# Window attention issued by pairs of steps, and later weight pieces, in an attention-and-router kernel

## The chip, the cores and the metric

One core of a Trainium2 chip runs the whole program. The metric is the device time of one execution in microseconds (us), and of several executions the median. Engines are named as in the profile: PE (TensorE matmul), DVE (VectorE), ACT (ScalarE), POOL (GpSimd), SP (SyncE, which here only issues DMAs).

## What is computed

The reference is an attention with a local window of 96 positions and 8 global keys, followed by a mixture of experts in which every token goes to one of 8 experts.

```
scores = q @ k.T / sqrt(D) - slopes * dist        # keep: key < 8, or 0 <= query - key < 96
a      = softmax(scores);  x = (a @ v) as (B*S, H*D)    # 4 batches, 8 heads, 768 positions, D 64
logits = (x / |x|) @ (emb / |emb|).T / tau        # 3072 tokens, 8 experts
e      = argmax(logits);  out = max(prob) * relu(x @ w1[e]) @ w2[e]     # 512 -> 1024 -> 512
```

All of it is float32.

## The kernel before

The program has two stages. In the first, `window_attention`, the 32 (batch, head) pairs are worked through in eight groups of four heads; two groups make a batch. Keys are cut in eight blocks of 96 rows, each with 30 rows of global keys under it (126 rows in all); a block with its queries is a unit, two units are a step, and four steps are a group, so there are 32 steps, numbered 0 to 31. In the last batch (steps 24 to 31) the steps of the two groups alternate. The order of PE, ACT, DVE and SP is the order in which the code is written; POOL's is left to a scheduler.

A step does the following on PE. `score` multiplies the keys and queries of its two units (32 small matmuls, L485) into two PSUM tiles a unit. `turn` transposes q and k of a coming group (three transposes a piece, L460), up to eight pieces a group. Then come the pieces of a half batch that is finished (`half_turns`): `turn_x` transposes a tile of 128 tokens (L587), `turn_sums` the row sums (L555), `turn_products` the experts' scores (L573), and `choose` counts the tokens of an expert (L219, L222). Last comes `attend` for the step before: exponentials times v (L514), and on every second step the row sums (L524), and, where a half batch is done, `score_experts` (L564).

Every PSUM tile for scores and transposes comes from `bank()`, which hands out five banks in turn, pa_121 to pa_125: whoever takes a bank waits until the engine that reads its former content is done. For scores that is ACT, which takes the exponential (`grow`, L491; DVE then multiplies by the window table, `weigh`, L498); for pieces of q and k it is ACT too (L462, L465, and the spread of the global keys, L467); for a token tile it is DVE (`store_x`, L596, which multiplies by the reciprocal row sums of L558 and so can't run before them); for the row sums DVE (L558), for the experts' scores DVE (L577, L579). `store_x` writes into one of three tiles xs, has SP store it to x_dram, and has ACT square it (L601). The squares go to POOL for a square root (`choose`, L226), from there to DVE (L236 to L238) and to ACT (L241).

SP issues, in program order, the loads of q, k and v of the group after the next (a quarter a step), the stores of xs, and the expert weights in pieces of 128 KB: from step 11 one in the middle and one at the end of each step. Expert 0 has 32 pieces (16 of w1, 16 of w2); the weights of expert 1 follow from step 27 on, when the tiles of q and k are given up.

The end of `window_attention` finishes the last half batch, issues what is left of expert 1's w1 with one call, `weights_part(count)`, and gives the rest to the second stage, which issues it behind the gathers of expert 0's tokens. The second stage runs the experts one after the other (gathers on POOL, products on PE).

Of the kernel before, what the change touches and what calls it, by code (L numbers as in the profile page):

```python
# [20 lines left out]
P = 128  # L21
# [11 lines left out]
BLK = 96  # L33
# [348 lines left out]
def window_attention(k, ctx):  # L382
# [5 lines left out]
    def pool(name, bufs, **kw):  # L388
# [5 lines left out]
    qk_p, tmp = (early.enter_context(tc.tile_pool(name=name, bufs=n, side="right"))  # L394
                 for name, n in (("wa_qk", 4), ("wa_tmp", 1)))
# [6 lines left out]
    k.junk, lS = (h[:, 0:2, :].rearrange("p f n -> p (f n)") for h in k.first.hT)  # L402
# [66 lines left out]
    def score(u):  # L469
# [5 lines left out]
        u.ex = (late_p if u.late else ex_p).tile([P, 2, 2, 2 * BLK], F32, name="ex", tag="ex")  # L475
# [24 lines left out]
    def attend(g, p, split=True):  # L500


        if p % 2 == 0:
            g.od = [po_p.tile([P, 512], F32, name="od%d" % i, tag="od%d" % i) for i in range(3)]
            k.free = g.od[2][:, QB * BLK :]
# [13 lines left out]
        g.parts = parts = (g.parts if p % 2 else []) + parts  # L519
        for u, at, c0, c1, first in parts if p % 2 else []:  # L520
            for a in range(2):
                for e in range(2):
# [3 lines left out]
                                     skip_group_check=True)  # L526
        if p % 2:
            xd = xd_p.tile([P, 2, QB * BLK], F32, name="xd", tag="xd")
            nc.scalar.copy(out=xd[:, 1, :], in_=g.od[1][:, 0 : QB * BLK])
            (nc.vector.tensor_copy if split else nc.scalar.copy)(out=xd[:, 0, :], in_=g.od[0][:, 0 : QB * BLK])  # L530
            g.xd.append(xd)
            h, den = p // 2, g.batch.den
            if g.m == 0:
                den[h] = den_p.tile([P, QB * BLK], F32, name="den", tag="den")
                nc.vector.tensor_copy(out=den[h][:], in_=g.od[2][:, 0 : QB * BLK])
            else:
                nc.vector.tensor_tensor(out=den[h][:], in0=g.od[2][:, 0 : QB * BLK], in1=den[h][:], op=ALU.add)
# [22 lines left out]
    def score_experts(hf, ps):  # L560
# [5 lines left out]
        nc.scalar.copy(out=lS[:, 0 : 3 * P], in_=ps[:, 0 : 3 * P])  # L566

    def turn_products(hf):
# [3 lines left out]
        for c in range(3):  # L572
            nc.tensor.transpose(ps[:, c * P : (c + 1) * P], lS[:, c * P : (c + 1) * P], k.ident[:])  # L573
# [47 lines left out]
    def half_turns(hf):  # L621
# [5 lines left out]
        elif hf.phase == 1:  # L627
# [4 lines left out]
        if hf.router and hf.phase == 1:  # L632
# [58 lines left out]
    for g in groups:  # L691
        g.units = []
        for j in range(NB):
            u = Net()
            u.g, u.j, u.n = g, j, (2 * BLK if j < NB - 1 else BLK)
            u.late = g.b == B - 1 and j == QB - 1
# [68 lines left out]
    waiting, active, k.root = [], [], []  # L765
    weights = [(0, i) for i in range(PIECES)]
    for s, (g, p) in enumerate(steps):
        if s % 8 == 0:
            before = t if s else None
            pair = groups[s // 4 : s // 4 + 2]  # L770
            t = new_batch(g.b)
            t.groups = pair
            for x in pair:
                x.batch = t
        ahead = s // 4 + 2
        if ahead < len(groups):
            if s % 4 == 0:
                open_group(groups[ahead])
            load_part(groups[ahead], s % 4)
        if s == len(steps) - 5:  # L780
            early.close()
            k.w.append(new_weights(k, k.second_weights()))
            weights.extend((1, i) for i in range(PIECES))

        def weights_part(n=1):
            for _ in range(n):
                if s >= 11 and weights:
                    e, i = weights.pop(0)
                    load_weights_part(k, e, k.w[e], i)

# [3 lines left out]

        us = g.units[2 * p : 2 * p + 2]
# [1045 lines left out]
```

## Time and profile before

| what | us |
|---|---|
| median of three runs | 512.15 |
| the three runs | 513.62, 508.52, 512.15 |
| the profiled execution, its own time | 511.49 |
| its span, first to last instruction | 509.8 |
| steps 4 to 23, scoring of step 4 to scoring of step 24 | 29.04 to 123.24 |
| steps 24 to 31, to the end of the last row sums on PE | 123.24 to 168.49 |

The span is the time between the first and the last instruction in the trace; 1.7 us of the execution's own time lie around it. Times in the rows below are microseconds from the start of the span. Matmuls overlap at their ends, so what a piece costs on PE is read from its start to the start of the next piece, not from its own length.

### The profile page before, as it was taken

How to read it: one execution, taken by the hardware profiler on the slowest of the kernel's cores; microseconds unless marked ns; L12 is line 12 of the kernel's file. 1: busy time of each engine (PE TensorE's matmuls, PEld its weight loads, DVE VectorE, ACT ScalarE, POOL GpSimd, SP SyncE). 2: the span in 40 equal slices, each digit the busy share in tenths (PEclk: the TensorE clock that was granted, in tenths of full speed). 3: DMA queues.
4: the chain of work that ended last, by engine and by line, in shares of the span. 5: the costliest groups of instructions: out<-in, count | busy, mean ns of one | idle time of the engine just before them, and what ended most of it. 6: DMA issues, size and time to landing. Idle time of an engine off the chain costs nothing.

```text
span 509.8 us, 13673 instructions
## 1 busy us (share of the span) xinstructions
PE 487.8 (96%) x5510; PEld 402.1 (79%) x5510; DVE 325.8 (64%) x642; ACT 183.2 (36%) x445; POOL 239.3 (47%) x265
## 2 busy tenths in 40 slices
PE   8999999999989898999999999999989989999995
PEld 7777887887867687969788579899779679859964
DVE  5646777766778565858569636777756664727531
ACT  4967867867654321402112111222212211312220
POOL 4211131333362526376736743865865764843022
PEclk9999999999999999999999999999998999999998
DMA  8999999799743636729561255284382274111001
GB/s 163 204 199 171 212 229 217 185 225 204 193 84 62 199 57 148 205 62 348 195 223 32 69 195 196 67 275 153 119 294 66 50 268 152 50 67 59 0 23 68
DMA packets 112863, 76.34 MB, mean 150 GB/s; under 512 B 88517, under 2 KB 96709, under 8 KB 112721
## 3 DMA queue, kind: packets, MB, share of 16 engines
q1 hardware_dynamic: 103057, 59.00, 44.1%
q0 software_dynamic: 8064, 15.27, 9.7%
q8 instruction: 63, 1.03, 0.9%
q14 instruction: 79, 0.65, 0.4%
q10 hardware_dynamic: 1600, 0.39, 0.4%
HBM read 61.66 MB, written 17.16 MB: 155 GB/s over the span
## 4 chain that ended last, share of the span: by engine, by line
PE 23%; issue 17%; POOL 13%; DMA 6%; POOLq 2%; DVE 1%; ACT 0%
PE big L1347 10%; POOL out_dram L1300 7%; DMA xg<-x_dram,squares 5%; POOL xg L1030 5%; PE big L1153 4%; PE work L1281 3%; PE big L1324 2%; PE work L1072 1%; PE work L1153 1%; POOLq L1806 1%; DMA xg<-x_dram,idss 1%; PE work L1062 0%; POOL landed L1029 0%; PE work L1294 0%; POOL xg L1003 0%
## 5 line engine op out<-in xcount | busy, mean ns | idle before, releaser
L1030 POOL DMA_INDIRECT xg<-x_dram,squares x96 | 107.1, 1116 | 62.5 <-issue 44.4
L498 DVE TENSOR_TENSOR ex<-ex,table 126x768 f32<-126x768 f32 x64 | 60.4, 950 | 36.7 <-ACT ex L491 36.5
L1347 PE MATMUL big<-xT,w1t 128*128 128x160 f32 (+4 forms) x336 | 61.2, 337 | 4.3 <-ACT hT L1371 2.3
L1347 PEld LDWEIGHTS big<-xT,w1t 128*128 128x128 f32 x336 | 56.4, 195 | 7.5 <-issue 2.8
L1357 DVE TENSOR_TENSOR hT<-big,hT 128x320 f32<-128x320 f32 (+4 forms) x70 | 38.4, 562 | 35.8 <-PE big L1347 26.7
L491 ACT ACTIVATE ex<-pa 126x384 f32<-126x384 f32 (+1 forms) x128 | 53.3, 477 | 16.4 <-PE pa L485 15.6
L261 POOL DMA_INDIRECT meta<-mt,slot x24 | 27.3, 1139 | 41.3 <-DVE rd L558 15.8
L514 PE MATMUL od<-ex,v 126*64 126x192 f32 (+1 forms) x576 | 46.0, 305 | 0.0
L1359 ACT ACTIVATE hT<-hT 128x320 f32<-128x320 f32 (+4 forms) x42 | 22.1, 531 | 57.1 <-DVE hT L1357 57.1
L514 PEld LDWEIGHTS od<-ex,v 126*64 126x64 f32 x576 | 34.7, 136 | 7.5 <-issue 3.5
L435 POOL COPY v<-v 30x896 f32<-30x896 f32 (+1 forms) x15 | 17.2, 1158 | 48.0 <-DMA v<-in_v_dram 28.5
L1347 PE MATMUL big<-xsum,fsum 128*128 128x160 f32 (+4 forms) x224 | 39.6, 330 | 0.0
L485 PE MATMUL pa<-qT,kT 64*32 64x128 f32 (+3 forms) x2048 | 38.2, 268 | 0.3 <-DVE xs L596 0.2
L485 PEld LDWEIGHTS pa<-qT,kT 64*32 64x32 f32 (+1 forms) x2048 | 29.7, 107 | 10.9 <-issue 7.2
L1347 PEld LDWEIGHTS big<-xsum,fsum 128*128 128x128 f32 x224 | 36.3, 190 | 1.7 <-DVE fsum L1117 0.4
L1300 POOL DMA_INDIRECT out_dram<-y_arm,tids x17 | 19.6, 1153 | 36.4 <-ACT y_arm L1283 31.8
L1281 PE MATMUL work<-w2t,hT 128*128 128x512 f32 x80 | 35.1, 593 | 0.0
L1153 PE MATMUL big<-wsum,hsum 128*128 128x256 f32 x136 | 31.2, 380 | 0.7 <-DVE hsum L1117 0.4
L1039 DVE STREAM_TRANSPOSE xT<-xg 128x512 f32<-128x512 f32 x24 | 25.3, 1082 | 7.6 <-DMA xg<-x_dram,squares 7.6
L1153 PEld LDWEIGHTS big<-wsum,hsum 128*128 128x128 f32 x136 | 25.7, 190 | 5.3 <-issue 1.1
L1153 PE MATMUL big<-w2t,hT 128*128 128x256 f32 x112 | 27.8, 386 | 1.3 <-DVE hsum L1118 1.0
L1281 PEld LDWEIGHTS work<-w2t,hT 128*128 128x128 f32 x80 | 15.1, 190 | 17.7 <-issue 17.6
(250 smaller groups left out, 871.1 us busy)
## 6 DMA issues: line engine op xcount, KB each, us to landing
w1t<-in_moe_w_dram SPq DMA_DIRECT2D x24, 512.0 KB, 7.4
w2t<-in_moe_w_dram SPq DMA_DIRECT2D x6, 2048.0 KB, 9.6
v<-in_v_dram SPq DMA_DIRECT2D x32, 192.0 KB, 4.4
x_dram<-xs SPq DMA_DIRECT2D x23, 256.0 KB, 4.7
k<-in_k_dram SPq DMA_DIRECT2D x28, 192.0 KB, 5.1
q<-in_q_dram SPq DMA_DIRECT2D x28, 192.0 KB, 5.5
w1t<-in_moe_w_dram SPq DMA_DIRECT2D x32, 128.0 KB, 5.8
w2t<-in_moe_w_dram SPq DMA_DIRECT2D x32, 128.0 KB, 3.4
```

What stands on the lines that cost most here:

```text
L261: i = nc.gpsimd.indirect_dma_start(out=k.meta[:], out_offset=bass.IndirectOffsetOnAxis(ap=slot[:, t : t + 1], axis=0), in_=mt[:, t, :], in ...
L485: i = nc.tensor.matmul(u.sp[e][k0:k1, a * n + c0 : a * n + c1], lhsT=t.kT[rows, j, k0:k1], rhs=t.qT[rows, j * BLK + c0 : j * BLK + c1], st ...
L491: nc.scalar.activation(u.ex[:, e], u.sp[e][0:ROWS, 0 : 2 * u.n].rearrange("p (a c) -> p a c", a=2), AF.Exp, scale=k.scale)
L498: nc.vector.tensor_tensor(out=exv, in0=exv, in1=tab[:, :, 0 : u.n // BLK, :], op=ALU.mult)
L514: nc.tensor.matmul(g.od[a][e * D : (e + 1) * D, at : at + c1 - c0], lhsT=g.v[0:ROWS, 2 * a + e, u.j, :], rhs=u.ex[:, e, a, c0:c1], start=f ...
L1030: k.nc.gpsimd.indirect_dma_start(out=xgs[j][:, g * P : (g + 1) * P], out_offset=None, in_=src, in_offset=bass.IndirectOffsetOnAxis(ap=ids[ ...
L1039: k.nc.vector.transpose(out=xT[:, :, :, j * half : (j + 1) * half].rearrange("p c a (g i) -> p g c a i", i=LACE), in_=xgs[j][:].rearrange( ...
L1153: i = self.k.nc.tensor.matmul(ps, lhsT=x[:, f, :], rhs=w[:, f, :], start=f == 0 and not add, stop=True, skip_group_check=True)
L1281: nc.tensor.matmul(ps[:], lhsT=hT[:, f, j * P : (j + 1) * P], rhs=w2[:, f, :], start=i == 0, stop=i == k.NF - 1)
L1300: i = k.nc.gpsimd.indirect_dma_start(out=k.out.rearrange("t (i m) -> (t i) m", i=n), out_offset=bass.IndirectOffsetOnAxis(ap=ids, axis=0), ...
L1347: nc.tensor.matmul(to[f // 2][:, f % 2 * 256 : f % 2 * 256 + h], lhsT=x[:, l, f * P : (f + 1) * P], rhs=y[:, l, 0:h], start=not (add or f ...
L1357: nc.vector.tensor_tensor(out=to, in0=x, in1=z, op=ALU.add)
```

## The change

Steps 4 to 23 are issued two at a time by a new function, `double`; steps 0 to 3 and 24 to 31 keep the old form, `single`. A double scores its first two units, does the values of the two steps of the double before, scores the other two, does the row sums, then the experts' scores if a half batch is done, then all pieces of q and k of both steps, then the pieces of finished halves. Where a step has its own pieces in the old form, a double does two token tiles in a row.

```
+    def double(s):
+        ...
+        score(us[0])
+        score(us[1])
+        exps(us[0])
+        exps(us[1])
+        done = [steps[i] for i in undone]
+        for q, qp in done:
+            values(q, qp)
+        copy_values(q, s < len(steps) - 10)
+        weights_part(s)
+        score(us[2])
+        scored = score(us[3])
+        scatter_later(k, 2, [scored] + k.root)
+        exps(us[2])
+        sums(q)
+        exps(us[3])
+        copy_sums(q, qp // 2)
+        undone[:] = [s, s + 1]
+        fresh = halves_done(done)
+        for x, a, i in turns[s] + turns[s + 1]:
+            turn(x.pairs[a], i)
+        for hf in active:
+            if hf.phase > hf.count:
+                half_router(hf)
+                hf.phase += 1
+                continue
+            for _ in range(2 if hf.h == 0 else 1 if hf.phase == 0 else 3):
+                half_turns(hf)
+                hf.phase += 1
+            if hf.router and hf.phase > hf.count:
+                next(hf.router)
+        active[:] = still(active) + fresh
+        weights_part(s)
+
+    for s in range(4):
+        single(s)
+    for s in range(4, 8 * (B - 1), 2):
+        double(s)
+    for s in range(8 * (B - 1), len(steps)):
+        single(s)
```

`attend` is cut into `values`, `sums`, `copy_values` and `copy_sums`, with the same instructions. The experts' scores have a buffer for each half, so that both can wait at once, and the products are turned right behind the row sums. Four units of a double and those of the double before need nine tiles ex in place of seven; two more come from the memory of the first tables.

```
-    k.junk, lS = (h[:, 0:2, :].rearrange("p f n -> p (f n)") for h in k.first.hT)
+    k.junk, *scored = (k.first.hT[i][:, j : j + 2, :].rearrange("p f n -> p (f n)") for i, j in ((0, 0), (1, 0), (1, 2)))
...
-        u.ex = (late_p if u.late else ex_p).tile([P, 2, 2, 2 * BLK], F32, name="ex", tag="ex")
+        more = k.spare is not None and u.n_th % 9 >= 7
+        u.ex = (late_p if u.late else k.spare if more else ex_p).tile([P, 2, 2, 2 * BLK], F32, name="ex", tag="ex")
...
         if hf.phase == 0:
             turn_sums(hf)
-        elif hf.phase == 1:
             turn_products(hf)
...
-            hf.router.send(bank() if hf.t.b >= B - 2 else k.free)
+            hf.router.send(bank())
```

The weights: a double issues two pieces (one a step), a single four. So 12 pieces go out in steps 12 to 23, 20 in steps 24 to 28, and 12 of expert 1 in steps 29 to 31. The call at the end of `window_attention` is not changed, but the function now takes the step first, and it issues nothing for steps under 11; the four pieces of expert 1's w1 that are left then fall to the second stage.

```
-        def weights_part(n=1):
+    def weights_part(s, n=1):
...
-        weights_part()
+        weights_part(s, 2)
...
     weights_part(sum(i < PIECES // 2 for e, i in weights))
```

What moves is seen first on PE. Before, this is step 16 behind its scoring: L460 are pieces of q and k, L587 a token tile, L573 the experts' scores, L514 and L524 the values and sums of step 15, and L485 the scoring of step 17.

```order
L460 MATMUL pa_122<-ident,k 128x128 x3
L460 MATMUL pa_123<-ident,q 128x128 x3
L587 MATMUL pa_124<-ident,xd 128x128 x4
L573 MATMUL pa_125<-ident,fhT_119 128x128 x3
L514 MATMUL od_1666<-ex,v 64x192 x2
L514 MATMUL od_1667<-ex,v 64x192 x2
L514 MATMUL od_1666<-ex,v 64x96 x2
L514 MATMUL od_1667<-ex,v 64x96 x2
L524 MATMUL od_1668<-ex,halves 32x96 x4
L524 MATMUL od_1668<-ex,halves 32x192 x12
L524 MATMUL od_1668<-ex,halves 32x96 x4
L485 MATMUL pa_121<-qT,kT 32x128
```

Now, on the same engine, this is the end of the double of steps 16 and 17: L581 are the experts' scores, L461 the four pieces, L604 the token tiles, L572 the row sums, L590 the turned scores, and L487 the first two matmuls of the next double's scoring.

```order
L581 MATMUL pa_125<-xd,enb 32x384 x4
L461 MATMUL pa_121<-ident,k 128x128 x3
L461 MATMUL pa_122<-ident,q 128x128 x3
L461 MATMUL pa_123<-ident,q 128x128 x3
L461 MATMUL pa_124<-ident,k 128x128 x3
L604 MATMUL pa_125<-ident,xd 128x128 x4
L572 MATMUL pa_121<-ident,den 128x128 x3
L590 MATMUL pa_122<-ident,fhT_119 128x128 x3
L604 MATMUL pa_123<-ident,xd 128x128 x4
L487 MATMUL pa_124<-qT,kT 32x128
L487 MATMUL pa_125<-qT,kT 32x128
```

Values and sums no longer stand between the transposes and the next scoring, and the second matmul of that scoring takes bank pa_125, the one of the first token tile. On DVE the same place reads, from the last two multiplications by the window table (L500) on: the copy of the sums (L547), reciprocals (L575), experts' scores (L594, L596), the two token tiles (L613), and the first units of the next double.

```order
L500 TENSOR_TENSOR ex<-ex,table 126x768 x2
L547 TENSOR_TENSOR den<-od_1717,den 128x384
L575 RECIPROCAL rd<-pa_121 128x3x4 x2
L594 TENSOR_TENSOR lh<-pa_122,rd 128x192
L596 TENSOR_REDUCE lg<-lh 128x24
L613 TENSOR_TENSOR xs<-pa_125,rd 128x512
L613 TENSOR_TENSOR xs<-pa_123,rd 128x512
L500 TENSOR_TENSOR ex<-ex,table 126x768 x2
```

The token tile in pa_125 is read behind the reciprocals and the experts' scores. On POOL, the place in the last batch where the square roots of batch 2's halves (L226, three columns) stand was this: copies of the global rows of v (L435) and stores of slots (L261) around them.

```order
L261 DMA meta<-mt_2352,slot_2347 28672x3 x3
L435 COPY v<-v 30x2x448
L261 DMA meta<-mt_2352,slot_2347 28672x3 x2
L435 COPY v<-v 30x2x448
L226 TENSOR_TENSOR ss<-ss,half 128x3
L261 DMA meta<-mt_2352,slot_2347 28672x3
L261 DMA meta<-mt_2786,slot_2781 28672x3 x2
L226 TENSOR_TENSOR ss<-ss,half 128x3
```

and is now this, with the copies of v ahead of the slots:

```order
L436 COPY v<-v 30x2x448 x2
L261 DMA meta<-mt_2401,slot_2396 28672x3 x6
L226 TENSOR_TENSOR ss<-ss,half 128x3 x2
L261 DMA meta<-mt_2859,slot_2854 28672x3 x3
L261 DMA meta<-mt_2954,slot_2949 28672x3 x3
```

No copy of v stands before the first square root any more, except those ahead of six stores of slots.

## Rows read from the trace of the kernel before

**Rows 1.** Busy time by stretch: start and end, its length, busy us (and count) of PE, PEld (weight loads), DVE, ACT, POOL, the granted PE clock, the DMA engines' busy share and GB/s.

```profile
29.04:123.24 94.20, 94.05 (x2270) 75.58 (x2268) 65.79 (x135) 65.90 (x173) 23.76 (x21) 1.00 0.94 208
123.24:164.28 41.04, 37.38 (x891) 29.34 (x887) 29.25 (x85) 25.67 (x69) 17.66 (x16) 1.00 0.53 120
...
383.50:386.90 3.40, 3.40 (x13) 3.40 (x12) 1.36 (x2) 0.49 (x1) 1.98 (x3) 0.50 0.20 58
```

**Rows 2.** Waits of PE between 29.04 and 164.28, the two longest: who waited for whom, us in all, times, the longest.

```profile
PE pa L219 <- ACT ex L491: 2.1, 1, 2.1
PE pa L587 <- ACT ex L491: 0.6, 1, 0.6
```

**Rows 3.** Timeline of PE: start, us, engine, line, operation, output<-inputs, shapes, count of records (two to a matmul), and the idle time before it with what ended it. Steps 8 and 9, the end of step 15, one row of step 30, and two of an expert.

```profile
46.60 1.13 PE L485 MATMUL pa<-qT,kT 64*32 64x128 f32 x64
47.66 0.55 PE L460 MATMUL pa<-ident,k 128*128 128x128 f32 x3
48.04 0.49 PE L460 MATMUL pa<-ident,q 128*128 128x128 f32 x3
48.37 0.60 PE L587 MATMUL pa<-ident,xd 128*128 128x128 f32 x4
48.81 0.49 PE L573 MATMUL pa<-ident,fhT 128*128 128x128 f32 x3
49.23 1.20 PE L514 MATMUL od<-ex,v 126*64 126x192 f32 x16
50.36 1.51 PE L524 MATMUL od<-ex,halves 126*32 126x96 f32 x40
51.80 1.13 PE L485 MATMUL pa<-qT,kT 64*32 64x128 f32 x64
...
54.10 1.52 PE L514 MATMUL od<-ex,v 126*64 126x192 f32 x16
55.55 1.13 PE L485 MATMUL pa<-qT,kT 64*32 64x128 f32 x64
...
83.97 0.85 PE L564 MATMUL pa<-xd,enb 128*32 128x384 f32 x8
84.75 1.19 PE L485 MATMUL pa<-qT,kT 64*32 64x128 f32 x64
...
156.97 0.66 PE L485 MATMUL pa<-qT,kT 64*32 64x128 f32 x32 [0.19 <-DVE xs L596]
...
382.77 4.55 PE L1347 MATMUL big<-xT,w1t 128*128 128x192 f32 x16 [2.29 <-ACT hT L1371]
387.15 2.76 PE L1347 MATMUL big<-xsum,fsum 128*128 128x192 f32 x16
```

**Rows 4.** Timeline of DVE, the same columns: a token tile of step 7, the experts' scores and a token tile of step 11, reciprocals and a token tile of step 29, and the sums of expert 1's w1.

```profile
44.74 0.69 DVE L596 TENSOR_TENSOR xs<-pa,rd 128x512 f32<-128x512 f32 x1 [0.20 <-DVE rd L558]
...
64.04 0.36 DVE L577 TENSOR_TENSOR lh<-pa,rd 128x192 f32<-128x192 f32 x1 [0.18 <-PE pa L573]
64.43 0.51 DVE L579 TENSOR_REDUCE lg<-lh 128x24 f32<-128x192 f32 x1
64.84 0.69 DVE L596 TENSOR_TENSOR xs<-pa,rd 128x512 f32<-128x512 f32 x1
...
155.89 0.30 DVE L558 RECIPROCAL rd<-pa 128x12 f32<-128x12 f32 x2
156.23 0.69 DVE L596 TENSOR_TENSOR xs<-pa,rd 128x512 f32<-128x512 f32 x1
...
214.31 1.16 DVE L1115 TENSOR_TENSOR fsum<-w1t 128x1024 f32<-128x1024 f32 x1
```

**Rows 5.** ACT by line and shape between 37 and 124: count, busy us, mean ns of one, idle time before.

```profile
L462 ACT COPY kT<-pa 128x384 f32<-128x384 f32 x19 | 9.7, 510 | 0.0
...
L467 ACT COPY kT<-kT 128x240 f32<-128x240 f32 x9 | 3.5, 393 | 0.3
```

**Rows 6.** Timeline of SP, whose rows are issues of DMAs: first load of step 4, what follows the loads of steps 4 and 5, the first store of a token tile, and the weights of expert 1 behind the gathers.

```profile
38.38 0.97 SPq L425 DMA_DIRECT2D k<-in_k_dram  x2
...
45.39 0.83 SPq L792 DMA_DIRECT2D x_dram<-zrow  x1
...
53.81 0.38 SPq L600 DMA_DIRECT2D x_dram<-xs  x1
...
201.59 9.97 SPq L182 DMA_DIRECT2D w2t<-in_moe_w_dram  x16
```

**Rows 7.** DMA issues by line: engine, count, KB each, median us from issue to landing.

```profile
x_dram<-xs SPq DMA_DIRECT2D x23, 256.0 KB, 4.7
...
w1t<-in_moe_w_dram SPq DMA_DIRECT2D x32, 128.0 KB, 5.8
```

**Rows 8.** Timeline of four engines in step 27, where PE waits longest.

```profile
141.07 0.93 POOL L435 COPY v<-v 30x896 f32<-30x896 f32 x1 [2.92 <-issue]
...
142.08 1.57 POOL L226 TENSOR_TENSOR ss<-ss,half 128x3 f32<-128x3 f32 x1
...
143.68 0.17 DVE L236 TENSOR_SCALAR ss<-ss 128x3 f32<-128x3 f32 x1 [0.78 <-POOL ss L226]
...
144.31 0.22 ACT L241 ACTIVATE lg<-lg 128x24 f32<-128x24 f32 x1 [2.28 <-DVE lg L238]
...
144.97 0.40 PE L219 MATMUL pa<-oh,prefix 128*128 128x24 f32 x2 [2.06 <-ACT ex L491]
```

More of the change, by code (lines that the diff above doesn't have):

```diff
@@ L498, in weigh, with open_sums, values @@
         nc.vector.tensor_tensor(out=exv, in0=exv, in1=tab[:, :, 0 : u.n // BLK, :], op=ALU.mult)
-    def attend(g, p, split=True):
+    def open_sums(g):
+        g.od = [po_p.tile([P, 512], F32, name="od%d" % i, tag="od%d" % i) for i in range(3)]
+        k.free = g.od[2][:, QB * BLK :]
+        g.parts = []
+    def values(g, p):
         if p % 2 == 0:
-            g.od = [po_p.tile([P, 512], F32, name="od%d" % i, tag="od%d" % i) for i in range(3)]
-            k.free = g.od[2][:, QB * BLK :]
+            open_sums(g)
         parts = []
@@ L526, in attend, with copy_values, copy_sums @@
                                      skip_group_check=True)
-        if p % 2:
[L528 to L537, printed above, removed]
+    def copy_values(g, split=True):
+        xd = xd_p.tile([P, 2, QB * BLK], F32, name="xd", tag="xd")
+        nc.scalar.copy(out=xd[:, 1, :], in_=g.od[1][:, 0 : QB * BLK])
+        (nc.vector.tensor_copy if split else nc.scalar.copy)(out=xd[:, 0, :], in_=g.od[0][:, 0 : QB * BLK])
+        g.xd.append(xd)
+    def copy_sums(g, h):
+        den = g.batch.den
+        if g.m == 0:
+            den[h] = den_p.tile([P, QB * BLK], F32, name="den", tag="den")
+            nc.vector.tensor_copy(out=den[h][:], in_=g.od[2][:, 0 : QB * BLK])
+        else:
+            nc.vector.tensor_tensor(out=den[h][:], in0=g.od[2][:, 0 : QB * BLK], in1=den[h][:], op=ALU.add)
+    def attend(g, p, split=True):
+        values(g, p)
+        if p % 2:
+            sums(g)
+            copy_values(g, split)
+            copy_sums(g, p // 2)
     def new_batch(b):
@@ L763, in window_attention, with begin_step @@
             turns[s].append(x)
-    waiting, active, k.root = [], [], []
+    active, undone = [], []
+    k.root, k.spare, k.batch = [], None, None
     weights = [(0, i) for i in range(PIECES)]
-    for s, (g, p) in enumerate(steps):
-        if s % 8 == 0:
[L769 to L774, printed above, removed]
+    def weights_part(s, n=1):
+        for _ in range(n):
+            if s >= 11 and weights:
+                e, i = weights.pop(0)
+                load_weights_part(k, e, k.w[e], i)
+    def begin_step(s, g):
+        if s % 8 == 0:
+            k.before, k.batch = k.batch, new_batch(g.b)
+            k.batch.groups = groups[s // 4 : s // 4 + 2]
+            for x in k.batch.groups:
+                x.batch = k.batch
         ahead = s // 4 + 2
@@ L779, in window_attention @@
             load_part(groups[ahead], s % 4)
+        if s == 4:
+            opening.close()
+            k.spare = early.enter_context(tc.tile_pool(name="wa_ex2", bufs=2, side="right"))
         if s == len(steps) - 5:
+            k.spare = None
             early.close()
@@ L793, in window_attention, with halves_done, still, single @@
             empty_slots(k)
+    def halves_done(done):
+        fresh = []
+        for q, qp in done:
+            if q.m == 1 and qp % 2:
+                fresh.append(start_half(q.batch, qp // 2))
+                score_experts(fresh[-1], bank())
+        return fresh
+    def still(hfs):
+        return [hf for hf in hfs if hf.phase < (hf.count + 2 if hf.router else 3)]
+    def single(s):
+        g, p = steps[s]
+        begin_step(s, g)
         us = g.units[2 * p : 2 * p + 2]
@@ L855, in window_attention @@
     scatter_later(k, len(k.later))
+    t, before = k.batch, k.before
     hf = start_half(t, 1)
```

47 lines of the change are left out of this document (25 added, 22 removed).

## The prediction

> **What bounds the kernel now.** I read the windows by stretch first. In steps 4 to 23, the part that the change rewrites, PE is busy 94.05 of 94.20 us at the full granted clock; DVE and ACT are busy some 66 us each, so each has 28 us to spare, but not always at the right moment [rows 1]. In the last batch PE is busy 37.38 of 41.04 us. The list of PE's waits says where: one wait of 2.1 us, one of 0.6, and smaller ones of about a microsecond together [rows 2]. So the first 20 steps are PE's own work in a row, and a change can win there only by making that work shorter, and lose by making PE wait where it never waited. The DMA engines are 94% busy in that stretch at 208 GB/s [rows 1], yet no wait of PE names a load.
>
> The timeline of PE gives the price of each piece, from its start to the next start [rows 3]: scoring 1.06 us (46.60 to 47.66), a piece of q or k 0.33, a token tile 0.44, row sums or turned scores 0.33, values of a second or fourth step 1.13 (49.23 to 50.36), of a first step 1.45 (54.10 to 55.55), row sums 1.44 (50.36 to 51.80), experts' scores 0.78.
>
> **What the change takes from PE.** It removes no instruction; it puts equal ones beside each other. From rows 3, what a border costs: the values of a first step have 8 matmuls of 192 columns and take 1.45; those of a second or fourth step have 4 of 192 and 4 of 96 and take 1.13. Two run at a time, so 2 x 96 columns cost 0.32, the shorter block's 6 x 96 cost 0.96, and 0.17 are paid once per block. The change joins ten pairs of such blocks (nine doubles, and step 24, which does two steps' values); the first double has one step's values to do. That is 10 x 0.17 = 1.7 us. For the transposes: the first in a group takes 0.38 and the last before values 0.42, where a middle one takes 0.33, so a group costs 0.14 more than its pieces. Steps 5 to 24 had 20 groups, the change leaves 11: 9 x 0.14 = 1.3 us. How transposes are followed by scoring directly is shown by no row; if that border costs the 0.17 of a values block and not 0.09, 11 x 0.08 = 0.9 us come back, and if nothing, another microsecond goes. Together -3.0 us, between -2.1 and -4.0.
>
> **Where PE will wait.** Now the cover that is gone. Before, values and sums (1.13 + 1.44 us) lay between the transposes and the next scoring, and in that time DVE read the token tiles out of their banks; PE never waited for it in steps 4 to 23. In a double, scoring comes directly behind, and it needs four of the five banks. Take the double of steps 16 and 17, times from the start of its transposes: four pieces to 1.37, first token tile 1.37 to 1.81 (bank pa_125), row sums to 2.14, turned scores to 2.47, second token tile to 2.91, and with 0.09 for the border scoring could begin at 3.00. DVE is free, but its chain starts with the row sums: three transposes end 0.49 after their start [rows 3], here at 2.30, and I allow 0.1 until DVE begins. Reciprocals 0.34, scores 0.39 and 0.41, tile 0.69 [rows 4]: 2.40, 2.74, 3.13, 3.54, 4.23. PE goes on 0.05 after a tile's end (156.23 + 0.69 against 156.97) [rows 3, 4], at 4.28, so it waits 1.28. The same double in batch 0 is that of steps 8 and 9.
>
> In the doubles of steps 10 and 18 the first token tile is that of the older half, whose reciprocals are known; the second comes behind the row sums. Counted as above from the start of the transposes: tiles at 1.37 and 1.81, row sums 2.25, scores 2.58, ready at 3.00; one unit scores (0.53), and the second unit wants the second tile's bank at 3.53. DVE: row sums end 2.74, reciprocals 2.84, scores 3.18 and 3.57, tile 3.98 to 4.67, PE at 4.72: a wait of 1.19. In steps 12 and 20 both tiles come early and the counting of tokens behind them covers DVE, so nothing. In 14 and 22 only pieces come: ACT copies them in 0.51 each and needs 0.39 for the spread [rows 5], each start a tenth or so ahead of the last one's end; the third is out at about 2.2, PE asks at 1.46 + 0.53 = 1.99: 0.2 to 0.3. Sum: 2 x 1.28 + 2 x 1.19 + 2 x 0.25 = +5.4 us. The lower bound is 0, as in the stretch now; the upper is 12.8, ten doubles at the longest wait. I take 5.4, since every part of it is a row and the order of the banks is written down.
>
> **Stores of token tiles.** They have three buffers. The tile of 44.74 was written by 45.43 and its store issued at 53.81 [rows 4, 6], since SP was still putting out loads: 8.4 us late. Landing takes 4.7 [rows 7], so a buffer may be held for 13.1 us. A double writes two tiles, so a buffer comes up again after 9.9 us in steps 8 to 10. There SP must put out the eight loads of steps 8 and 9 first, 6.9 us by those of steps 4 and 5 (38.38 to 45.3) [rows 6], behind the 53.8 at which it is done with the older ones: store at 60.7, landed at 65.4. With the doubles of steps 4 and 6 some 14.2 us long, the next user of the buffer comes at about 64.3. That is +0.9 on DVE and so on PE, between 0 and 3.3. Later SP has less to do, since the doubles carry 12 pieces of weights instead of 26: 14 x 128 KB is 1.8 MB or 9 us at 208 GB/s.
>
> **The last batch.** The wait of 2.06 in step 27 is read backwards [rows 8]: counting waits for a bank, that for an exponential on ACT, ACT stands behind L241 until 144.31, that waits for DVE, DVE at 143.68 for the square root on POOL, and POOL began it at 142.08 because a copy of v stood before it in its order and ended at 142.00. The change has no copy of v there, and takes this half one step later, so the square root has a step's time. I count the wait as gone: -2.06, bounds 0 and -2.06. Of the smaller waits of steps 28 to 31, which hang on the same late square roots, half: -0.5, bounds 0 and -1.0. The 0.6 in step 24 stays: four pieces and a token tile follow its scoring as before.
>
> **The weights** I cost at nothing. Expert 0's last piece goes out in step 28, 30 us before its sums; expert 1's last four pieces of w1 go out behind the gathers, from 201.59 on, 0.62 each (9.97 / 16), and land 5.8 later [rows 6, 7], at about 210; DVE wants them at 214.31 [rows 4]. If that cover is gone, every microsecond beyond some 216 is one on the end. The second stage is otherwise untouched and moves as a whole.
>
> **Sum.** -3.0 + 5.4 + 0.9 - 2.06 - 0.5 = +0.7 us. On the profiled execution's 511.49 that is 512.2; its time is 0.66 under the median of the three runs, which themselves lie 5 us apart, so this is a forecast of no change. About 1%, 5.1 us, is what a measurement of this kernel can tell.
>
> **Rivals.** First, faster: the bank waits don't come, since DVE gets to the tiles sooner than my chain, and all small waits of the last batch go: -3.0 - 2.06 - 1.0, which gives 505.4. For it speaks that DVE and ACT are idle for 30% of that stretch; against it the order, in which the tile stands behind four operations that cannot begin before the row sums. Second, slower, by the stores: if SP stays as late as at 53.81, a buffer is held 13.1 us and wanted after 9.8, so DVE stands still for 3.3 us and PE behind it. At steps 10 and 18 that makes 6.6 in place of 0.9: 517.9; also at 12 and 20 it would be 525. It decides from the point where SP is over 5 us behind when the tiles are written. For it speaks the DMA share of 94%; against it the lighter weights.
>
> Third, the clock. The granted clock was 0.50 between 383.50 and 386.90 [rows 1], after PE had been idle for 2.29 us up to 382.77; the block that followed took 4.38 us where the next has 2.76 [rows 3], some 1.7 lost. The idle time of 2.06 in step 27 stood in a stretch granted 1.00, so a wait of 1.3 alone should not do it. But such a wait would now follow 3 us of transposes. Four such drops cost 4 x 1.7 = 6.8: 519.0. The Trainium skill (TensorE: Matmul & The Clock Gate, Part 4: PE-mode transpose) says that transposes don't count as busy for the clock in the same way; by that rule the doubles of steps 8, 10, 16 and 18 would lower it. The wait of 0.6 behind the transposes of step 24 [rows 2] fell in a stretch granted 1.00 [rows 1], so the trace bears the rule out little so far. Fourth, the late pieces of w1 land after 216 and hold up expert 1: up to some 5 us, 517.
>
> **How the numbers follow.** Forecast 0.60, faster rival 0.20, stores 0.13, clock 0.04, weights 0.03. Two thirds of the faster rival lie beyond 1%, and a twentieth of the forecast on each side: faster 0.17. Slower: most of the stores, the clock, half of the weights and that twentieth: 0.18. The rest, 0.65, is within 1%. The range reaches to the faster rival and just over the cheaper form of the second and the clock: 505 to 520; the forecast's own range is 508 to 516.
>
> **What would show it.** In the trace after: no wait of PE for a load; waits of scoring for DVE's token tile, about 1.2 to 1.3 us, in the doubles of steps 8, 10, 16 and 18 and none in 12 and 20; DVE never idle for a buffer but once near 64; the step-27 wait gone; the granted clock 1.00 up to the second stage; steps 4 to 24 some 3 us longer and the rest of the batch some 2.5 shorter. The forecast is wrong if the doubles run without waits, if DVE waits for stores, or if the second stage changes its length by over 2 us.

## The result, and the profile after

The changed kernel takes 515.11 us (median of 20 runs, 511.43 to 518.72), the kernel before, beside it, 512.22 (20 runs, 508.52 to 517.51): a ratio of 1.0063, 95% interval 1.0038 to 1.0088, so some 3 us more. The forecast was 512.2, between 505 and 520, with no change beyond 1% as the likeliest case. The time lies there, but 2.9 us over the forecast, and in the two profiles the excess comes mainly from one place that the forecast's sum doesn't hold.

First the two windows that answer to [rows 1]: steps 4 to 23, and from there to the last values; then the stretch on PE behind its longest wait.

```profile
28.72:124.77 96.05, 90.34 (x2239) 74.67 (x2237) 64.52 (x124) 65.16 (x169) 21.68 (x20) 1.00 0.93 197
124.77:165.06 40.29, 39.57 (x920) 31.44 (x919) 31.60 (x97) 27.27 (x75) 15.56 (x16) 1.00 0.60 133
175.09:181.06 5.97, 5.93 (x19) 4.92 (x20) 2.81 (x9) 3.24 (x8) 3.06 (x4) 0.52 0.74 265
```

Steps 4 to 23 went from 94.20 to 96.05 us, with PE idle for 5.7 of them where it was idle for 0.15; the next stretch from 41.04 to 40.29. The waits of PE, as in [rows 2], name the places:

```profile
PE pa L487 <- DVE xs L613: 4.4, 4, 1.2
PE pa L691 <- DVE xs L613: 3.0, 1, 3.0
...
PE od L531 <- issue: 1.2, 1, 1.2
```

The first row is the four waits that were forecast. This is PE's timeline at the ends of the doubles of steps 8 and 10 (compare the steps of [rows 3]):

```profile
53.40 0.60 PE L604 MATMUL pa<-ident,xd 128*128 128x128 f32 x4
53.84 0.49 PE L572 MATMUL pa<-ident,den 128*128 128x128 f32 x3
54.17 0.49 PE L590 MATMUL pa<-ident,fhT 128*128 128x128 f32 x3
54.50 0.60 PE L604 MATMUL pa<-ident,xd 128*128 128x128 f32 x4
55.03 0.40 PE L487 MATMUL pa<-qT,kT 64*32 64x128 f32 x2
56.43 1.11 PE L487 MATMUL pa<-qT,kT 64*32 64x128 f32 x62 [1.00 <-DVE xs L613]
...
65.23 0.65 PE L487 MATMUL pa<-qT,kT 64*32 64x128 f32 x32
67.06 0.66 PE L487 MATMUL pa<-qT,kT 64*32 64x128 f32 x32 [1.19 <-DVE xs L613]
```

In the first double one matmul of the next scoring gets through and the second stands; in the other a whole unit gets through. Both are as the order of the banks said, and steps 16 and 18 repeat them (1.00 and 1.19). DVE's side of the first wait, in the order of [rows 4]:

```profile
54.44 0.32 DVE L575 RECIPROCAL rd<-pa 128x12 f32<-128x12 f32 x2 [1.59 <-PE pa L572]
54.89 0.36 DVE L594 TENSOR_TENSOR lh<-pa,rd 128x192 f32<-128x192 f32 x1
55.28 0.50 DVE L596 TENSOR_REDUCE lg<-lh 128x24 f32<-128x192 f32 x1
55.70 1.28 DVE L613 TENSOR_TENSOR xs<-pa,rd 128x512 f32<-128x512 f32 x2
```

DVE stands idle for 1.59 us for the row sums, then runs the chain, tile last.

The wait of 2.06 in step 27 [rows 8] is gone: both counts of tokens stand behind a tile without a gap.

```profile
142.07 0.30 PE L219 MATMUL pa<-oh,prefix 128*128 128x24 f32 x2
...
147.41 0.30 PE L219 MATMUL pa<-oh,prefix 128*128 128x24 f32 x2
```

What no part of the forecast has is the tail, behind the last values. PE there, before:

```profile
170.24 1.04 PE L587 MATMUL pa<-ident,xd 128*128 128x128 f32 x8
172.52 1.09 PE L675 MATMUL pa<-ident,xg 128*128 128x128 f32 x8 [1.24 <-DVE xs L596]
173.44 0.49 PE L573 MATMUL pa<-ident,fhT 128*128 128x128 f32 x3
174.33 1.99 PE L683 MATMUL pa<-fxT,w1t 128*128 128x256 f32 x8 [0.40 <-ACT fxT L676]
```

and after:

```profile
171.02 1.04 PE L604 MATMUL pa<-ident,xd 128*128 128x128 f32 x8
175.09 1.97 PE L691 MATMUL pa<-ident,xg 128*128 128x128 f32 x8 [3.04 <-DVE xs L613]
176.86 0.84 PE L590 MATMUL pa<-ident,fhT 128*128 128x128 f32 x3
177.74 3.49 PE L699 MATMUL pa<-fxT,w1t 128*128 128x256 f32 x8
```

PE comes 0.77 us later and waits 3.04 in place of 1.24; then its clock is granted at half (0.52 in the third window above), and the same rows, up to the rest of the first products, take 6.78 us (175.09 to 181.87) in place of 4.86 (172.52 to 177.38). That is 1.80 + 1.92 = 3.7 us. What DVE waits for there is a square root on POOL; POOL's timeline, before:

```profile
156.64 0.96 POOL L261 DMA_INDIRECT meta<-mt,slot  x1 [3.54 <-PE pa L564]
157.90 0.96 POOL L261 DMA_INDIRECT meta<-mt,slot  x1 [0.30 <-issue]
159.17 1.53 POOL L261 DMA_INDIRECT meta<-mt,slot  x1 [0.30 <-issue]
165.58 0.19 POOL L668 CAST ids<-emt 128x4 int32<-128x4 f32 x1 [4.88 <-DMA emt<-meta]
166.57 1.02 POOL L1003 DMA_INDIRECT xg<-x_dram,ids  x1 [0.80 <-POOL ids L668]
167.89 0.97 POOL L1003 DMA_INDIRECT xg<-x_dram,ids  x1 [0.30 <-issue]
168.88 0.90 POOL L226 TENSOR_TENSOR ss<-ss,half 128x3 f32<-128x3 f32 x1
```

and after:

```profile
157.66 0.96 POOL L261 DMA_INDIRECT meta<-mt,slot  x1 [1.70 <-issue]
158.92 0.96 POOL L261 DMA_INDIRECT meta<-mt,slot  x1 [0.30 <-DVE m L205]
160.18 0.96 POOL L261 DMA_INDIRECT meta<-mt,slot  x1 [0.31 <-issue]
161.45 0.96 POOL L261 DMA_INDIRECT meta<-mt,slot  x1 [0.30 <-DVE ex L500]
168.15 0.19 POOL L684 CAST ids<-emt 128x4 int32<-128x4 f32 x1 [5.74 <-DMA emt<-meta]
169.14 1.02 POOL L1088 DMA_INDIRECT xg<-x_dram,ids  x1 [0.81 <-DMA w1t<-in_moe_w_dram]
170.46 0.97 POOL L1088 DMA_INDIRECT xg<-x_dram,ids  x1 [0.30 <-issue]
171.45 0.90 POOL L226 TENSOR_TENSOR ss<-ss,half 128x3 f32<-128x3 f32 x1
```

The slots (L261) of batch 2's second half must be stored, loaded again (emt) and cast before the first gathers (L1088) can go, and the square root stands behind those. All of it is 2.57 us later: four slots stand in the last row in place of three, since the older half of that batch is now taken a step later. The load of the slots on SP, before and after:

```profile
163.69 0.38 SPq L993 DMA_DIRECT2D emt<-meta  x1
...
166.04 0.38 SPq L1078 DMA_DIRECT2D emt<-meta  x1
```

From the start of step 29's scoring PE reaches the wait 20.18 us later before (151.10 to 171.28) and 17.95 after (154.10 to 172.05); the first gather starts 15.47 and 15.04 behind it. PE got 2.2 us shorter there, the chain 0.4.

### The profile page after: what moved, and what is told of

It reads as the page before. It is cut to its first block, busy times and chain, and to the rows that moved or that the text cites. A ratio compares the mean times of both kernels' runs of the same rounds, so it can differ in the third digit from the quotient of the medians.

```text
span 513.1 us, 13684 instructions
## 1 busy us (share of the span) xinstructions
PE 486.7 (95%) x5510; PEld 404.2 (79%) x5510; DVE 326.8 (64%) x642; ACT 184.4 (36%) x445; POOL 239.0 (47%) x265
## 3 DMA queue, kind: packets, MB, share of 16 engines
q8 instruction: 63, 1.03, 0.9%
## 4 chain that ended last, share of the span: by engine, by line
PE 44%; issue 6%; POOL 5%; DMA 4%; DVE 1%; POOLq 1%; ACT 0%; ACTq 0%
PE big L1432 21%; PE big L1238 9%; PE work L1366 7%; POOL out_dram L1385 3%; PE work L1238 3%; POOL xg L1115 2%; DMA xg<-x_dram,squares 2%; PE big L1409 2%; PE work L1379 1%; PE work L1157 1%; DMA out_dram<-y,idss 1%; DMA xg<-x_dram,idss 1%; PE work L1147 0%; POOLq L1891 0%; POOL landed L1114 0%
## 5 line engine op out<-in xcount | busy, mean ns | idle before, releaser
L1115 POOL DMA_INDIRECT xg<-x_dram,squares x96 | 105.9, 1104 | 60.9 <-issue 42.2
L500 DVE TENSOR_TENSOR ex<-ex,table 126x768 f32<-126x768 f32 x64 | 58.9, 951 | 30.2 <-ACT ex L493 30.0
L493 ACT ACTIVATE ex<-pa 126x384 f32<-126x384 f32 (+1 forms) x128 | 50.8, 479 | 5.9 <-PE pa L487 3.7
L261 POOL DMA_INDIRECT meta<-mt,slot x24 | 26.1, 1089 | 40.6 <-DVE mt L260 12.9
L520 PE MATMUL od<-ex,v 126*64 126x192 f32 (+1 forms) x576 | 43.8, 303 | 0.0
L487 PE MATMUL pa<-qT,kT 64*32 64x128 f32 (+3 forms) x2048 | 39.3, 264 | 4.6 <-DVE xs L613 4.4
L487 PEld LDWEIGHTS pa<-qT,kT 64*32 64x32 f32 (+1 forms) x2048 | 29.0, 105 | 13.5 <-DVE xs L613 5.7
```

Source lines behind the costliest of these rows:

```text
L261: i = nc.gpsimd.indirect_dma_start(out=k.meta[:], out_offset=bass.IndirectOffsetOnAxis(ap=slot[:, t : t + 1], axis=0), in_=mt[:, t, :], in ...
L487: i = nc.tensor.matmul(u.sp[e][k0:k1, a * n + c0 : a * n + c1], lhsT=t.kT[rows, j, k0:k1], rhs=t.qT[rows, j * BLK + c0 : j * BLK + c1], st ...
L493: nc.scalar.activation(u.ex[:, e], u.sp[e][0:ROWS, 0 : 2 * u.n].rearrange("p (a c) -> p a c", a=2), AF.Exp, scale=k.scale)
L500: nc.vector.tensor_tensor(out=exv, in0=exv, in1=tab[:, :, 0 : u.n // BLK, :], op=ALU.mult)
L1115: k.nc.gpsimd.indirect_dma_start(out=xgs[j][:, g * P : (g + 1) * P], out_offset=None, in_=src, in_offset=bass.IndirectOffsetOnAxis(ap=ids[ ...
```

## Experiments

The stages below are cut at the scoring of steps 4, 24 and 31 and at the first product of the second stage; us, from one profile each.

| kernel | to step 4 | 4 to 23 | 24 to 30 | 31 and tail | second stage | ratio to before (95%) |
|---|---|---|---|---|---|---|
| before | 29.04 | 94.20 | 38.40 | 40.92 | 307.24 | 1 |
| after | 28.72 | 96.05 | 37.85 | 44.48 | 306.00 | 1.0063 (1.0038 to 1.0088) |
| e1 | 28.50 | 95.57 | 38.30 | 43.92 | 302.71 | 1.0036 (1.0004 to 1.0068) |
| e2 | 28.86 | 96.52 | 37.95 | 45.58 | 306.09 | 1.0061 (1.0028 to 1.0093) |
| e3 | 28.75 | 96.44 | 37.56 | 44.86 | 302.89 | 1.0044 (1.0012 to 1.0076) |
| e4 | 28.63 | 98.76 | 36.99 | 47.62 | 303.50 | 1.0047 (1.0013 to 1.0080) |
| e11 | 28.82 | 97.00 | 38.03 | 45.48 | 303.17 | 1.0038 (1.0003 to 1.0073) |
| e12 | 28.79 | 97.44 | 37.92 | 42.99 | 302.26 | 1.0050 (1.0018 to 1.0082) |

The medians are 514.79 us for e1, 515.60 for e2, 515.18 for e3 and 515.29 for e4 beside 512.21, and 513.20 for e11 and 514.16 for e12 beside 511.28. The second stage, which no edit touches, differs by 5 us from profile to profile. In the three with 306 us or more the granted clock fell to 0.50 for 3.4 us in that stage (from 383.50 before, 389.00 after and 391.60 in e2); in the other five it stayed at 1.00. That drop cost 1.7 us in the kernel before [rows 1, 3]; the rest of the difference is not explained. So the intervals tell the edits apart hardly at all, and what follows rests on the stages. Each is read from one execution, which may lie some us from its kernel's median (e1's took 510.75, e12's 511.17).

**e1.** One slot more in step 28.

```
-        scatter_later(k, 1 if s < len(steps) - 8 else 2 if s < len(steps) - 3 else 3, ...)
+        scatter_later(k, 1 if s < len(steps) - 8 else 2 if s < len(steps) - 4 else 3, ...)
```

> The changed kernel, but step 28 issues three scatters of slots in place of two, so that none is left for the end of step 29. Theory A (the +3.7 us behind the last values come from POOL: one slot scatter more there, 1.26 us by 160.18 to 161.45, makes the load of the slots, the two gathers and with them the square root late): the gathers start 1.3 us earlier, about 167.9 in place of 169.14, and PE's wait before the turning of the gathered rows (3.04) is about 1.8. If PE then still falls to half clock, 513.8; if not, another 2.0 us go (5.97 us in place of 3.95 for the same rows), 511.8. Rival W (the weights, which SP now issues in larger lots in the tail, make it late): the wait stays 3.0 and the time 515.1.

The third slot went out at 156.00. Against the start of step 29's scoring (153.84 here, 154.10 in the changed kernel) the last slot began 0.96 us earlier, but it took 1.73 us in place of 0.96 and landed nearly as late as before: the load of the slots went 0.15 us earlier, and the first gather began at 168.88, 15.04 behind that scoring as in the changed kernel. The wait stayed 3.02. The edit did not move the gathers, which theory A needed moved, so it speaks neither for nor against it.

**e2.** The square root ahead of the gathers on POOL.

```
+        for x in k.root:
+            k.tc.add_manual_dep(i.ins, x.name, ..., reason="behind the square root")
```

> The changed kernel, but on POOL the last square root but one stands ahead of the two gathers of the first rows, no other engine's order changed. Theory B (the square root behind the gathers is what is late): it runs at 167.2 as soon as ACT's squares are there, DVE's chain ends the first token tile at 172.6 in place of 175.04, PE waits 0.6 in place of 3.04 and the clock stays: 515.1 - 2.4 - 2.0 = 510.7. Theory A (the slots are late, and the gathers with them): PE then waits for the gathered rows, 169.14 + 5.2 (a gather's landing in the kernel before) = 174.3, a wait of 2.3: 514.3, or 512.3 if that keeps the clock up.

PE now waits for the gathers themselves:

```profile
174.72 0.63 PE L693 MATMUL pa<-ident,xg 128*128 128x128 f32 x4 [1.95 <-DMA xg<-x_dram,ids]
177.10 1.09 PE L693 MATMUL pa<-ident,xg 128*128 128x128 f32 x4 [1.75 <-DMA xg<-x_dram,ids]
```

3.7 us in two waits. Theory B falls: behind the square root the landing of the gathered rows is just as late. Both hang on the slots. The time, 515.60, is over theory A's 514.3 too, which had 2.3 us for these waits.

**e3.** DVE's token tile ahead of the experts' scores.

```
             turn_sums(hf)
-            turn_products(hf)
         if xp is not None:
             store_x(t, i, xp)
+        if hf.phase == 0:
+            turn_products(hf)
```

> The changed kernel, but DVE reads the token tile of a half's first phase before it works on the experts' scores, not behind (PE's order unchanged). Theory (PE waits for DVE's chain in four doubles): the waits of 1.00, 1.19, 1.00, 1.19 shrink by the two operations taken out of the chain, 0.36 + 0.41 = 0.8 each: 0.2, 0.4, 0.2, 0.4, and the time by 3.2 us to 511.9. Rival (something else sets the place, or the time is given back in the last batch, whose experts' scores come 0.7 later): the waits or the time stay, 515.1.

In the doubles of steps 8 and 16 no idle time is left, in that of step 18 0.29: DVE's chain is what PE waits for. In step 10 the wait grew to 1.52. DVE says why:

```profile
63.94 0.32 DVE L575 RECIPROCAL rd<-pa 128x12 f32<-128x12 f32 x2
65.52 0.69 DVE L613 TENSOR_TENSOR xs<-pa,rd 128x512 f32<-128x512 f32 x1 [1.26 <-DMA x_dram<-xs]
```

The tile's buffer is still being stored, which the chain had covered. The stage did not get shorter (96.44): PE stopped three times in the row sums, 3.5 us in all, and no row names a cause (the last section comes back to it):

```profile
34.30 0.49 PE L531 MATMUL od<-ex,halves 126*32 126x192 f32 x9 [0.96 <-issue]
...
111.08 1.50 PE L531 MATMUL od<-ex,halves 126*32 126x96 f32 x35 [1.83 <-issue]
...
122.78 0.29 PE L531 MATMUL od<-ex,halves 126*32 126x96 f32 x4 [0.69 <-issue]
```

**e4.** No doubles.

```
-    for s in range(4, 8 * (B - 1), 2):
-        double(s)
+    for s in range(4, 8 * (B - 1)):
+        single(s)
-        weights_part(s, 2)          # both places
+        weights_part(s, 2 if s >= 8 * (B - 1) else s % 2)
```

> The changed kernel with steps 4 to 23 issued by singles, one piece of weights a step there as in doubles; the last batch, the tail, the buffers of experts' scores and the order of the turned scores stay as changed. Theory (pairing saves 2.6 us of borders and costs 4.4 us of waits for a token tile's bank): no wait for a token tile in steps 4 to 23, 94 us for them as in the kernel before, 515.1 + 2.6 - 4.4 = 513.3, and 512.1 if PE's unexplained stop of 1.24 us in the first double goes too; the wait of 3.0 in the tail stays. Rival (pairing is what pays, and the loss is in the last batch and tail alone): 517.7 or more.

No wait for a token tile in that stage, as expected, but 98.76 us for it in place of 94. Summed from start to next start without the idle time, the experts' scores take 5.63 us (3.87 before), pieces 16.04 (14.56), tiles 6.84 (6.07): in the new order some of these stand inside the groups, by the releasers in the trace for a bank that ACT reads or for copied values. So this is not the old kernel with one part of the change: both theories fall here, and up to step 31 pairing, with all its waits, takes 1.9 us off that order (135.75 to 133.90 from step 4 on). The tail is longest here (47.62; gathers landed 7.2 us after their issue), so its loss doesn't need the doubles.

**e5 to e8.** When these and e9 and e10 ran, the kernel before took 537 us. In their profiles steps 24 to 30 take 44 to 50 us (37.85 in the changed kernel) and the second stage 318 to 339, with stops of PE for which no row shows a cause. Only what doesn't hang on those stops is read from them.

```
         for hf in active:                            # e5, e7, e8
             half_turns(hf)
+            if s == 8 * (B - 1) and hf.h == 0:
+                hf.phase += 1
+                half_turns(hf)
-        weights_part(s, 2)          # both places; e6, e7, e8
+        weights_part(s, 2 if s < len(steps) - 3 else 1)
-    weights_part(sum(i < PIECES // 2 for e, i in weights))
+    weights_part(len(steps) - 1, sum(i < PIECES // 2 for e, i in weights))
```

e8 has e3's edit as well.

> The changed kernel, but in step 24 the older half of batch 2 takes two of its phases (its first two token tiles, the row sums and the scores), as in a double, so that its square root, its choice and its slots come a step earlier, as in the kernel before. Theory H (the tail's 3.7 us come from the half taken a step later: its slots are still on POOL when those of the next half are due, so the load of slots, the two gathers and the square root behind them are late): the older half's last slot is out before 154 in place of 156 to 158, the last slot of all some 1.2 us earlier, first gather about 167.7, PE's wait ahead of the gathered rows 1.8 or less in place of 3.04; time 513.9, and 511.9 if the clock then stays up. Rival W (landing times behind the heavier weights of the last steps): the wait stays near 3, 515.1.

> The changed kernel, but from step 29 on two pieces of weights a step in place of four, and the call at the end of the first stage issues the 10 that are left of expert 1's w1 there, behind the stores, as the kernel before does. Rival W: slots, load of slots and gathers land about 1 us sooner (0.6 in the load of slots by its distance from the last slot, 3.6 in place of 3.0), and PE's wait shrinks from 3.04 to 2 or less; with the clock up 512. Theory H: the gathers start at most 0.6 earlier, the wait stays near 2.5 to 3 and the time at 514.5 to 515.1. The second stage's length stays the same by both.

> Both edits of the two runs before, the older half's two phases in step 24 and the weights held back from step 29 on. If both causes count, the tail is that of the kernel before: PE's wait ahead of the gathered rows 1.2 to 1.5, no half clock there, first gather some 2.3 us earlier against PE; 515.1 - 3.7 = 511.4. If only one counts, no better than that one alone.

> The same, and DVE reads the token tile ahead of the experts' scores: the waits in four doubles go from 4.4 to 1.8 us or less, as seen in the profile with that edit alone (none in two doubles, 0.3 and 1.5 in the others). If stops of PE that no row explains (3.5 us in that profile, in the row sums) do not take their place: 511.4 - 2.6 = 508.8, below the kernel before. If they do, 511 to 512.

Times: e5 543.17, e6 548.24, e7 540.48, e8 544.03 beside 536.63; ratios 1.019 (0.997 to 1.041) for e5, 1.031 (1.021 to 1.041) for e7, 1.017 (0.996 to 1.037) for e8, none for e6. All four miss the wait that they were to move: PE comes so late to the gathered rows that it waits 0.5 us, whatever was edited, and runs on at the full clock. What they do show is the way from the last slot's end on POOL to the cast: 4.56, 4.77 and 4.02 us in e6, e7 and e8, which hold the weights back, and 5.57 in e5, which doesn't. In the kernel before it is 4.88, in the changed kernel 5.74. So the heavier weights seem to cost the slots and their load about 1 us, as rival W had it; what PE's wait would become without them is not shown for the kernel as it is. Taking two phases in step 24 costs PE a new wait of 1.9 for DVE's count.

**e9 to e12.** The slots of steps 28 and 29 and the router's work as early as PE's order lets them; e10 and e12 with e3's edit.

```
+        early_slots = len(steps) - 4 <= s <= len(steps) - 3
+        if early_slots:
+            scatter_later(k, 3, [scored] + k.root)
         grow(us[0], 0)
...
-        fresh = halves_done(done)
         for hf in active:
             half_router(hf)
             hf.phase += 1
+        fresh = halves_done(done)
```

> The changed kernel with PE's order unchanged; on ACT and DVE the router's work of a half stands ahead of the next half's experts' scores, and in steps 28 and 29 the slots (three in each) stand ahead of the multiplications by the window table. Theory H (the chain from batch 2's second choice over slots, load of slots, gathers and square root sets the tail, and what the last batch gains on PE before it is lost there): last slot out about 159.7 in place of 162.4, first gather 166.5 in place of 169.1, PE's wait ahead of the gathered rows 0.4 to 1.2 in place of 3.04, no half clock in the first products: 515.1 - 2.2 - 2.0 = 510.9, at least 513 if the gathers' landing (4.5 to 5.7) takes over. Rival (DVE's own work or the landings set it): wait near 3, 515.

> The same, and DVE reads the token tile ahead of the experts' scores, which took the waits of four doubles from 4.4 to 1.8 in a profile. If both gains stand: 510.9 - 2.6 = 508.3, under the kernel before by 0.7%. If PE's stops in the row sums that no row explains (3.5 us with that edit alone) take the place of the waits: 511 to 512.

> The kernel of the earlier slots once more, since PE stopped for 10 to 20 us at places that no row explains when it ran first, and the kernel before took 537 us there. Where the kernel before takes 512: Theory H: last slot out about 159.7, first gather 166.5, PE's wait ahead of the gathered rows 0.4 to 1.2 in place of 3.04, the first products at full clock: 510.9 (513 if the gathers' landing takes over). Rival: wait near 3, 515.

> The kernel of the earlier slots and of the token tile ahead of the experts' scores once more, for the same reason. Where the kernel before takes 512: the waits of four doubles 1.5 to 1.8 in place of 4.4 and the tail as in the run beside it: 508.3, under the kernel before by 0.7%; 511 to 512 if PE's stops in the row sums take the place of the waits.

e9 took 533.47 and e10 540.41 beside 537.45 (e9's ratio 0.993, 0.987 to 0.998; none for e10). Later, when the kernel before took 511.28, the same two, as e11 and e12, took 513.20 and 514.16: e9's small lead did not come again, and neither is faster than the kernel before. In e11 the last slot ended 6.6 us after step 29's scoring began (8.3 in the changed kernel), but the load of the slots and its cast then took longer:

```profile
160.93 0.96 POOL L261 DMA_INDIRECT meta<-mt,slot  x1 [0.30 <-DVE best L211]
168.39 0.19 POOL L684 CAST ids<-emt 128x4 int32<-128x4 f32 x1 [6.51 <-DMA emt<-meta]
```

6.5 us from the last slot's end to the cast, where it was 5.7 (162.41 to 168.15), and PE waited 2.70 and 1.02 more for the gathers' landing. Theory H's edit moved the slots; most of the gain was lost in the transfers behind them: of 1.74 us at the last slot's end 0.98 are left at the first gather and 0.29 where PE goes on. e12, with the same slots, has 6.6 us to the cast as well, but PE went on 6.15 us after the start of the first gather (6.64 in e11): it waited 2.07 and 0.36, and its tail of 42.99 is the shortest of the changed ones. e12 shows one more price:

```profile
63.86 0.65 PE L487 MATMUL pa<-qT,kT 64*32 64x128 f32 x32
66.46 0.66 PE L487 MATMUL pa<-qT,kT 64*32 64x128 f32 x32 [1.94 <-DVE xs L613]
67.05 4.51 PE L520 MATMUL od<-ex,v 126*64 126x96 f32 x40
```

```profile
66.00:71.00 5.00, 4.54 (x64) 3.58 (x66) 4.68 (x10) 2.24 (x6) 1.94 (x2) 0.66 1.02 225
```

The store of a tile held DVE for 1.68 us there, PE waited 1.94 behind transposes, the clock fell, and values that take 2.83 us elsewhere took 4.51.

## Why the prediction was right, and where not

**Borders, -3.0.** Start to next start, without idle time, the values of steps 4 to 23 went from 27.45 to 24.32. Of that 1.78 is the block of step 22, now done in step 24; it is a third step's block, longer than the two that the prediction prices. PE before:

```profile
120.67 1.85 PE L514 MATMUL od<-ex,v 126*64 126x96 f32 x24
122.45 0.85 PE L564 MATMUL pa<-xd,enb 128*32 128x384 f32 x8
```

So the nine doubles saved 1.35, and the pair in step 24 takes 2.76 in place of 1.78 and 1.13: 1.5 in all, 0.15 for each of ten (forecast 1.7, at 0.17). Transposes went from 24.41 to 22.27, 0.77 of it a tile and row sums that moved: 1.4 (1.3). Together 2.9: right.

**Bank waits, +5.4.** Idle 4.38, forecast 4.94 for the four; another 1.5 inside the scorings (21.83 to 23.37), where 0.5 were forecast. These stand not only where they were forecast: the scorings of steps 6, 8 and 16, behind transposes alone, take 1.37 to 1.48 in place of 1.06, and 0.2 to 0.4 come on top of each of the four waits. No waits in steps 12 and 20. Together 5.9: right, and e3 shows the cause of the four.

**Stores, +0.9.** Not in the changed kernel: the tile's wait covered it. e3 and e12 uncover it, 1.26 and 1.68 near 65, and only there, as forecast for that buffer.

**The last batch, -2.06 and -0.5.** From step 24 to the scoring of step 31 the time fell by 0.55 with 2.55 us of work more in it (the block of values, the tile and the row sums): 3.1, of which 0.15 is counted with the borders. PE's idle time there fell from 3.66 to 0.64: the wait of step 27 went, and of the small ones all but the one in step 24 that was forecast to stay. So 3.0 in place of 2.56; half of the small waits was too little. The moved work is one reason why steps 4 to 23 grew by 1.85 and not by some 3, and steps 24 to 30 fell by 0.55 and not by some 2.5.

**PE's stop of 1.24** in step 4's row sums was not forecast. e1 shows no idle time of this kind, other profiles of doubles up to 3.5, the kernel before 0.15 in that stage.

**The step that failed** is in the sum, and in the sentence that the second stage "moves as a whole": all that the last batch gains was taken to arrive at the end. The tail already waited 1.24 and 0.40, so a chain beside PE ended there: slots, load of slots, gathers and square root on POOL, token tile. That chain was given work (one slot, a half a step later) while PE was relieved. Its 2.57 us are 1.03 until the slots' numbers are written by DVE (155.70 to 156.73), 0.68 of slots on POOL, 0.64 until the load can go (163.69 and 166.04 on SP) and 0.22 in the load. With the half clock it costs 3.7. Borders, waits, last batch and tail make -2.9 + 5.9 - 2.95 + 3.7 = +3.75, near the 2.9 of the medians (PE's stop and a second stage 1.2 us shorter cancel between the two profiles). The forecast's own terms, as measured, make zero where it had +0.7. That the forecast comes so near to that is in part luck, since the stores stayed out while the waits and the gain of the last batch were each 0.4 to 0.5 larger than forecast.

That the slots set the tail is shown by the two traces and by e2, where each strand takes the other's place. That earlier slots give the time back was tried (e1, e11, e12) and is not shown, or at most in part: from the last slot's end to the cast 5.9, 6.5 and 6.6 us passed, where it was 5.7, and the tail took 43.92, 45.48 and 42.99 us beside 44.48 after and 40.92 before. The 0.64 and the 0.22 lie in DMAs that land beside the weights, which the forecast costed at nothing. In the profiles of kernels that issue fewer weights there (before, e6, e7, e8) the way from slot to cast takes 4.0 to 4.9 us, in all others 5.6 to 6.7. (POOL's ends are rough: from the last slot's start it is 6.41 us before and 6.70 after.) So that second term probably failed too, by up to about 1 us; how much of the time it is stays open.

**Clock.** Waits of 1.0 to 1.5 us behind transposes left it at 1.00, and so did the 2.06 of step 27 before the change, behind one token tile; those of 1.94 (e12) and 3.04 (the tail) did not, and the price was 1.7 and 1.9, near the figure of the third rival. The Trainium skill (TensorE: Matmul & The Clock Gate, Part 4: PE-mode transpose) says that transposes don't count as busy for the clock in the same way. By the traces that may be so: in the second stage, behind matmuls, waits of 1.98 (e12), 2.27 (e11) and 2.77 (e4) kept the full clock, but 2.09 (e2), 2.29 [rows 3] and 2.44 (after) lost it, so it doesn't decide alone, and neither does the length of the wait.

**The rivals** did not come as told: the first, since the waits came; the second and the fourth, since neither DVE nor the second stage waited (306.0 in place of 307.24); the third's drop of the clock came in the tail and not in the doubles.

## What to carry to other kernels

When a reordering gives PE time, follow every chain that ends at the next place where PE waits already, however small that wait: there PE is no longer what decides, and its gain is lost beyond that wait. Where work is moved a step later, look for the last thing that is built on it (here a slot list, loaded again from memory), not only for PE's own wait at the old place. A wait of 2 to 3 us can cost nearly 2 us more in the clock of the matmuls behind it, as it did here in e12 and in the tail, but not every such wait does.

## What was not expected of the hardware

PE's stops without a named cause came in dense rows of small matmuls (40 records in 1.4 us), in stretches with the DMA engines at a share of 1.0 to 1.2. They do not go by the waits for a bank: 1.24 us in the changed kernel, 1.8 in e11 and none in e1, which have the waits, and 3.5 in e3 and 2.7 in e12, where two of the four are gone.

The traces say more than the rows above. In all 14 profiles every stop of 0.4 us or more in steps 4 to 23 stands at one of the same three places of PE's program, behind its 599th, 2379th or 2633rd matmul record; even the 0.15 of the kernel before does. And each of them ended 1.24 to 1.49 us after a 16 KB transfer of a DMA queue that the profile calls instruction had landed: at 33.08 for the stop up to 34.54 in the changed kernel, at 109.79 for the one up to 111.08 in e3. So PE most likely stood for its own next instructions, whose load shares the DMA engines with the program's data; no run was made to test this. The stops of 0.2 to 0.8 us in the scorings of the last steps, seen in every profile of e5 to e10, have no such regular landing ahead of them, and their cause stays open.
